# A tuned attention and mixing kernel: another hand-written order for the steps of its first two units

## The chip, the cores and the metric

One core of a Trainium2 chip runs the whole program in one launch. The metric is the device time of that launch in microseconds (us), as the median over several runs. The runs of the kernel before took 1000.03 to 1002.81 us, with a median of 1001.09 us.

## The reference

Three blocks follow each other. Only the first two are touched by the change.

```python
# 1: attention within chunks of 64, batch 8, 8 heads, sequence 576, head width 64
scores = q_c @ k_c.T / sqrt(64);  attn = softmax(scores);  out = attn @ v_c
# 2: the heads side by side give x (8, 576, 512); x_prev is x one step earlier
xk = mu_k * x + (1 - mu_k) * x_prev;  xr = mu_r * x + (1 - mu_r) * x_prev
k = relu(xk @ w_k)                        # 512 -> 1024
v = (k * k) @ w_v                         # 1024 -> 512
x2 = sigmoid(xr @ w_r) * v
# 3: four causal attention experts over x2 with a top-2 gate, width 64 each
```

## The kernel before

**Tiles and units.** Blocks 1 and 2 run as one pipeline. The 4608 positions (batch times sequence) are cut into 36 tiles of 128 for the attention and into 12 units of 384 for the mixing. Two neighbouring tiles make a pair: pair 0 is tiles 0 and 1, the seventh pair (pair 6) is tiles 12 and 13. The units are counted from 0, so the third unit is unit 2. Tiles from 12 on are loaded in 32 by 32 blocks (eight DMAs for a tile of q or of k) and transposed by VectorE; earlier tiles are loaded by one or two DMAs and transposed by TensorE.

**Precision.** Each float32 operand of a mixing product is split into a high and a low part, and each term is three matmuls (lines 95 to 97). One product step is 12 matmuls of 128x384.

**The order.** The scheduler does not choose the order of this part. Two lists of steps, START (line 21) for units 0 and 1 and TWO_UNITS (line 46) for each later two units, are walked by `follow` (line 495), and `in_line` (line 485) ties each instruction to the one before it on its engine. So the place of a step in the list is its place in the queue of every engine that it uses, SP's DMA queue too. An engine waits at the head of its queue for whatever that instruction still needs. The change is in START alone. The steps, as the lists name them:

- `L A G B H O` i: load a 512 KB piece of the weights on SP (L420), then split it into high and low: A on ScalarE (L426), G on VectorE (L430 and L431), B on VectorE (L435), H on GpSimd (L84), O on VectorE (L446). Pieces 0 to 3 are w_r, 4 to 11 w_k, 12 to 19 w_v. Pieces 4 and later share two staging buffers; one is free again after a B.
- `lq lk lv` t: load a tile of q, k or v on SP (L151 and L158, L166 and L174). Two buffers each; the v buffers of a pair are free after `V` of that pair, the q and k buffers after the tile's transposition.
- `Tq Tk Tp` t: transpose on TensorE (L187), or on VectorE (L197) for q and k from tile 12 on; `Eq Ek Ep`: copy out of PSUM on ScalarE (L192).
- `S X U E Z Y V W` j: attention of pair j. S (L211, L214) and V (L267, L270) are TensorE's; X (L224), U (L230), Z and Y are VectorE's; E and W are ScalarE's.
- `a b c d`, with `r` or `k`, u,g: the four stages of one shift of unit u (xr or xk), on ScalarE (L304), VectorE (L308), ScalarE (L315), VectorE (L319). They share two buffers.
- `r s` u,m: product with w_r, sigmoid. `k K J` u,m: product with w_k, three ScalarE instructions from L364 on (relu, square, high part), low part on VectorE (L370). `v y z x D` u,m: product with w_v in two halves, multiplication, split and store. The products of r, k and v share three PSUM banks.

TWO_UNITS follows START at once. Its first steps, for units 2 and 3 and from tile 12 on, are

```python
TWO_UNITS = """
Tq1 Tq0 lq2 Tk1 k0,0 Tk0 prev1 ar1,3 ak1,0 k0,1 br1,3 K0,0 bk1,0 lk2 cr1,3 k0,2 J0,0 K0,1 dr1,3 ar1,0 J0,1 k0,3 K0,2
```

so there `k0,0` is unit 2's first product with w_k, and the four `T` steps transpose tiles 12 and 13 on VectorE. START has made unit 2's r products and its shifts already.

Of the kernel before, what the change touches and what calls it, by code (L numbers as in the profile page):

```python
# [18 lines left out]
F64_BIAS = 2.0 ** -112  # L19

START = """
L7 A7 G7 B7 L3 G3 L5 H7 O7 A3 B3 H3 lk0 L6 lq0 Tq0 L1 A5 G5 B5 L14 H5 lk1 Tk0 O3 A6 G6 B6 lq1 Eq0 L2 Tk1 H6 O5 G1 O6
A1 B1 A14 Ek1 G14 H1 O1 lk2 B14 H14 Ek0 G2 O14 Tq1 Eq1 S0 mu A2 B2 X0 H2 O2 lk3 L4 A4 Tk2 Ek2 U0 E0 G4 Z0 lq2 Tq2 lq3
Eq2 Tk3 lv1 B4 Y0 Tq3 L11 G11 H4 Ek3 Eq3 S1 X1 A11 B11 H11 Tp1 Ep1 U1 lv0 Tp0 O11 Ep0 lq5 Tq5 lq4 V0 O4 E1 Z1 Y1 W0 L0
Tq4 A0 lk5 G0 lk4 Tk5 L8 G8 Ek5 B0 Eq5 Eq4 H0 Tk4 Ek4 Tp3 Ep3 Tp2 Ep2 S2 X2 lv2 O0 lv3 L19 A8 V1 W1 prev0 U2 A19 G19
ar0,2 br0,2 ar0,0 br0,0 E2 Z2 cr0,2 dr0,2 lq7 Tq7 lk6 Tk6 Eq7 cr0,0 dr0,0 Y2 lq6 Tq6 Eq6 lk7 Tk7 Ek6 ar0,1 br0,1 ar0,3
Ek7 br0,3 cr0,1 lq8 Tq8 Tp4 B8 Ep4 lk8 S3 cr0,3 H8 Eq8 dr0,1 ak0,2 Tk8 Ek8 Tp5 lq9 Tq9 dr0,3 r0,0 r0,1 X3 bk0,2 lv5
ak0,1 Ep5 bk0,1 Eq9 U3 O8 ck0,2 ck0,1 lk9 Tk9 B19 H19 lv4 V2 dk0,1 dk0,2 E3 Z3 lq11 Tq11 s0,1 r0,2 r0,3 Ek9 S4 ak0,0
bk0,0 ak0,3 bk0,3 W2 prev1 ck0,3 ck0,0 L10 s0,3 G10 dk0,3 A10 s0,2 lk10 s0,0 dk0,0 k0,0 k0,1 k0,2 O19 L9 G9 B10 H10
ar1,0 lv7 br1,0 A9 B9 lk11 Tk11 lq10 Tq10 H9 Eq11 O10 L17 Y3 K0,0 O9 K0,1 J0,1 L18 cr1,0 dr1,0 A17 ar1,1 lk13 K0,2 G17  # L30
J0,0 ar1,2 A18 k0,3 Tp6 Ep6 br1,1 G18 k0,4 J0,2 lv6 k0,5 B18 H18 Tp7 cr1,1 K0,4 dr1,1 B17 O18 H17 J0,4 ar1,3 K0,3
br1,2 cr1,2 br1,3 k0,6 k0,7 cr1,3 K0,6 L13 A13 L12 O17 J0,3 K0,7 dr1,2 dr1,3 r1,0 r1,1 G13 A12 Ep7 B13 H13 Eq10 s1,0
L15 G12 B12 Ek11 V3 O13 J0,7 G15 s1,1 H12 O12 A15 W3 B15 L16 r1,2 Tk10 r1,3 A16 G16 Ek10 S5 s1,2 H15 O15 K0,5 B16 H16
lv9 ak1,1 J0,6 J0,5 s1,3 v0,0,0 O16 v0,0,1 ak1,3 bk1,3 X4 v0,1,0 v0,1,1 ck1,3 v0,2,0 v0,2,1 bk1,1 ck1,1 dk1,1 U4 ak1,0
E4 bk1,0 y0,1 z0,1 x0,1 D0,1 y0,0 dk1,3 ak1,2 bk1,2 ck1,0 dk1,0 v0,3,0 ck1,2 dk1,2 v0,3,1 k1,0 K1,0 z0,0 x0,0 y0,2
z0,2 D0,0 k1,1 K1,1 Z4 Y4 Tp9 Tp8 Ep8 y0,3 lv8 X5 J1,1 U5 k1,2 k1,3 x0,2 Ep9 K1,2 k1,4 k1,5 J1,2 D0,2 J1,0 K1,3 J1,3
K1,4 z0,3 x0,3 k1,6 k1,7 E5 J1,4 K1,5 K1,6 J1,5 K1,7 v1,0,0 J1,6 V4 W4 J1,7 v1,0,1 prev2 v1,1,0 ak2,1 D0,3 lv11 v1,1,1
v1,2,0 v1,2,1 Z5 Y5 Tp10 bk2,1 y1,0 ar2,2 br2,2 v1,3,0 cr2,2 v1,3,1 z1,0 y1,1 x1,0 D1,0 dr2,2 ar2,0 br2,0 ck2,1 dk2,1
cr2,0 dr2,0 ar2,3 br2,3 ar2,1 br2,1 Ep10 cr2,3 z1,1 x1,1 D1,1 Tp11 dr2,3 y1,2 z1,2 cr2,1 dr2,1 r2,0 r2,1 x1,2 ak2,3
bk2,3 ck2,3 dk2,3 s2,0 ak2,2 y1,3 ak2,0 s2,1 r2,2 r2,3 z1,3 lv10 Ep11 V5 s2,2 x1,3 D1,3 bk2,0 ck2,0 s2,3 bk2,2 ck2,2  # L40
lv13 lk12 D1,2 W5 lq13 lv12 lq12 dk2,0 dk2,2
""".split()

CH = 64
# [999 lines left out]
```

## Time and profile before

| | before |
|---|---|
| median of three runs | 1001.09 us |
| the profiled execution | 1000.0 us, of which its span 998.0 us |
| TensorE matmul busy | 946.5 us (95%) |
| VectorE, ScalarE, GpSimd busy | 670.2, 624.0, 192.2 us |
| span, DMA | 108.38 MB, mean 109 GB/s |

The execution's time stands beside the span that its trace covers; the 2 us between them lie outside the trace. Times in the rows count from the start of the span. PE is TensorE's matmul, DVE VectorE, ACT ScalarE, POOL GpSimd, SP the engine that issues most DMAs. A row names the line, the operation, the tile written and the tile read; "idle before" is what the engine waited just before that instruction and what ended the wait.

### The profile page before, as it was taken

What the parts mean: (1) busy time and instruction counts of PE and PEld (TensorE: products, weight loads), DVE (VectorE), ACT (ScalarE), POOL (GpSimd) and SP (SyncE); (2) the same over time, 40 slices, a digit from 0 to 9 for tenths busy, and PEclk for the clock granted to TensorE, in tenths of its full rate; (3) what the DMA queues carried; (4) which work ended last, traced back from release to release, by engine and by line L of the source; (5) the groups of instructions that cost most, each with busy time, mean ns of one, the idle gap of its engine ahead of it and who ended that gap; (6) DMA issues with size and microseconds to landing.
All of it is one profiled execution on the core that took longest, in us unless ns stands there. A gap on an engine that the chain in (4) does not pass through costs nothing.

```text
span 998.0 us, 21524 instructions
## 1 busy us (share of the span) xinstructions
PE 946.5 (95%) x8022; PEld 908.4 (91%) x8022; DVE 670.2 (67%) x1705; ACT 624.0 (63%) x1417; POOL 192.2 (19%) x336
## 2 busy tenths in 40 slices
PE   2699998699999999999999999999999999999997
PEld 2589998699999999999999999989989998998996
DVE  7899552565665557464747622688786787778885
ACT  3588364547675675657466924476675667567675
POOL 3112111020201111020202024323321233222101
PEclk9699999799999999999999999999999999999999
DMA  9875123453344334433413225565453645354312
GB/s 255 201 193 145 44 69 85 67 109 71 96 77 93 81 86 86 85 92 74 107 30 85 49 69 138 117 171 135 112 156 94 179 87 174 87 170 137 100 44 97
DMA packets 223408, 108.38 MB, mean 109 GB/s; under 512 B 187352, under 2 KB 199752, under 8 KB 223304
## 3 DMA queue, kind: packets, MB, share of 16 engines
q1 hardware_dynamic: 193032, 67.16, 29.7%
q0 software_dynamic: 30272, 39.86, 14.7%
q8 instruction: 63, 1.03, 0.4%
q14 instruction: 41, 0.34, 0.1%
HBM read 66.01 MB, written 28.38 MB: 95 GB/s over the span
## 4 chain that ended last, share of the span: by engine, by line
PE 84%; DVE 8%; DMA 3%; SPq 1%; ACT 1%; issue 1%; POOL 0%; ACTq 0%; POOLq 0%; DVEq 0%
PE mps L95 17%; PE mps L97 16%; PE mps L96 16%; PE pj L95 6%; PE pj L96 6%; PE pj L97 6%; PE Sps L747 4%; PE Tps L807 3%; PE AVps L840 2%; PE Tps L187 2%; PE AVps L836 2%; DMA st<-in_moe_w_k_dram 2%; PE PVps L267 1%; PE Sps L211 1%; DVE PTl L814 1%
## 5 line engine op out<-in xcount | busy, mean ns | idle before, releaser
L95 PE MATMUL mps<-xhk,wkh 128*128 128x384 f32 x384 | 131.9, 343 | 11.9 <-ACT r L364 11.9
L96 PE MATMUL mps<-xlk,wkh 128*128 128x384 f32 x384 | 129.9, 338 | 0.0
L97 PE MATMUL mps<-xhk,wkl 128*128 128x384 f32 x384 | 129.8, 338 | 0.0
L95 PE MATMUL mps<-kh,wvh 128*128 128x384 f32 x384 | 129.3, 338 | 0.0
L97 PE MATMUL mps<-kh,wvl 128*128 128x384 f32 x384 | 128.4, 334 | 0.0
L96 PE MATMUL mps<-kl,wvh 128*128 128x384 f32 x384 | 128.3, 334 | 0.0
L370 DVE TENSOR_TENSOR kl<-r,kh 128x384 fp32r<-128x384 f32 x96 | 54.0, 564 | 100.0 <-ACT kh L366 100.0
L759 ACT ACTIVATE P<-sm,nm 128x512 f32<-128x512 f32 (+3 forms) x144 | 83.7, 583 | 22.2 <-DVE nm L749 13.4
L84 POOL CAST x2d<-x2o 128x384 fp32r<-128x384 f32 x48 | 31.3, 653 | 316.1 <-DVE x2o L387 314.0
L749 DVE CUSTOM_DVE_ANT_0 sm<-Sps,mask 128x256 f32<-128x256 f32 (+4 forms) x160 | 74.8, 478 | 21.6 <-PE Sps L747 20.7
L95 PEld LDWEIGHTS mps<-xhk,wkh 128*128 128x128 f32 x384 | 73.0, 190 | 12.9 <-ACT r L364 12.5
L814 DVE TENSOR_TENSOR PTl<-Tps,PTh 128x512 fp32r<-128x512 f32 (+2 forms) x144 | 70.3, 506 | 5.8 <-ACT PTh L813 4.4
L96 PEld LDWEIGHTS mps<-xlk,wkh 128*128 128x128 f32 x384 | 73.0, 190 | 0.0
L97 PEld LDWEIGHTS mps<-xhk,wkl 128*128 128x128 f32 x384 | 72.9, 190 | 0.0
L95 PEld LDWEIGHTS mps<-kh,wvh 128*128 128x128 f32 x384 | 72.0, 188 | 0.7
L96 PEld LDWEIGHTS mps<-kl,wvh 128*128 128x128 f32 x384 | 72.1, 188 | 0.0
L97 PEld LDWEIGHTS mps<-kh,wvl 128*128 128x128 f32 x384 | 72.1, 188 | 0.0
L304 ACT ACTIVATE xa<-XT,mu 128x384 f32<-128x384 f32 x96 | 57.0, 615 | 23.4 <-DVE xlk L319 12.3
L308 DVE SCALAR_TENSOR_TENSOR xa<-XT,mu,xa 128x384 f32<-128x384 f32 x96 | 57.6, 621 | 18.4 <-ACT xa L304 18.1
L364 ACT ACTIVATE r<-mps 128x384 f32<-128x384 f32 x96 | 46.6, 485 | 34.5 <-PE mps L97 34.1
L813 ACT ACTIVATE PTh<-Tps 128x512 fp32r<-128x512 f32 (+2 forms) x144 | 61.7, 454 | 8.5 <-PE Tps L807 6.8
L95 PE MATMUL mps<-xhr,wrh 128*128 128x384 f32 x192 | 66.3, 345 | 0.0
(182 smaller groups left out, 2629.9 us busy)
## 6 DMA issues: line engine op xcount, KB each, us to landing
x2T<-x2d POOLq DMA_DIRECT2D x48, 384.0 KB, 2.8
x<-x2T POOLq DMA_DIRECT2D x32, 576.0 KB, 7.0
K<-Kph SPq DMA_DIRECT2D x64, 128.0 KB
out_dram<-o SPq DMA_DIRECT2D x32, 256.0 KB
ldk<-in_k_dram SPq DMA_DIRECT2D x192, 32.0 KB
ldq<-in_q_dram SPq DMA_DIRECT2D x192, 32.0 KB
ldv<-in_v_dram SPq DMA_DIRECT2D x21, 256.0 KB
st<-in_moe_w_k_dram SPq DMA_DIRECT2D x8, 512.0 KB
```

Source lines behind the costliest of these rows:

```text
L95: nc.tensor.matmul(out=out, lhsT=ah, rhs=bh, start=first and i == 0, stop=False)
L96: nc.tensor.matmul(out=out, lhsT=ah, rhs=bl, start=False, stop=False)
L97: nc.tensor.matmul(out=out, lhsT=al, rhs=bh, start=False, stop=last and i == n - 1)
L304: nc.scalar.activation(out=a, in_=XT[u][:, g, :, :SEG], func=ACTF.Copy, scale=mu1[:, w, g:g + 1])
L308: nc.vector.scalar_tensor_tensor(a, XT[u][:, g, :, 1:], mu[:, w, g:g + 1], a, op0=ALU.mult, op1=ALU.add)
L364: nc.scalar.activation(out=r, in_=MB.pop(("k", u, m)), func=ACTF.Relu)
L370: eng(nc, CFG["klo"][u >= CFG["nearly"]]).tensor_tensor(o.lo, K2.pop((u, m)), f32(o.hi), op=ALU.subtract)
L747: issued = nc.tensor.matmul(out=pp[:, :w], lhsT=x, rhs=y[:, a:a + w], start=n == 0, stop=n == len(terms) - 1)
L749: nc.vector.tensor_tensor_reduce(out=sm[:, a:a + w], in0=pp[:, :w], in1=mk[:, :w], op0=ALU.add, op1=ALU.min, scale=-scale, scalar=3e38, ac ...
L759: nc.scalar.activation(out=x[:, :nk], in_=sm[:, :nk], func=ACTF.Exp, scale=-1.0, bias=nm[:, :1], accum_out=z)
L813: nc.scalar.activation(out=h, in_=src, func=ACTF.Copy)
L814: nc.vector.tensor_tensor(l, src, f32(h), op=ALU.subtract)
```

## The change

The list START is written in another order. It has the same 502 steps, each once; no step is added, dropped or altered, and everything after the list is the same. The first and the last lines of the two versions:

```diff
-L7 A7 G7 B7 L3 G3 L5 H7 O7 A3 B3 H3 lk0 L6 lq0 Tq0 L1 A5 G5 B5 L14 H5 lk1 Tk0 O3 A6 G6 B6 lq1 Eq0 L2 Tk1 H6 O5 G1 O6
...
-bk2,3 ck2,3 dk2,3 s2,0 ak2,2 y1,3 ak2,0 s2,1 r2,2 r2,3 z1,3 lv10 Ep11 V5 s2,2 x1,3 D1,3 bk2,0 ck2,0 s2,3 bk2,2 ck2,2
-lv13 lk12 D1,2 W5 lq13 lv12 lq12 dk2,0 dk2,2
+L3 G3 A3 L0 A0 B3 G0 H3 O3 B0 L4 G4 H0 O0 L1 A4 B4 H4 L15 G15 O4 A15 lq0 B15 lk1 G1 H15 O15 A1 B1 H1 Tk1 L7 G7 A7 lk0
...
+ak2,1 bk2,1 ck2,1 dk2,1 lq12 z1,1 x1,1 D1,1 Ep10 ak2,3 y1,3 s2,0 s2,1 r2,2 V5 r2,3 bk2,3 ck2,3 ak2,0 lv12 bk2,0 dk2,3
+z1,3 x1,3 D1,3 lv13 ck2,0 W5 s2,2 s2,3 dk2,0
```

**First place: SP's queue at the end of the list.** Before, the last loads of START and the first of TWO_UNITS; v tiles 11, 10 and 13, k 12, q 13, v 12, q 12, and then q 14 (k tile 13 stands far ahead of them):

```order
L174 DMA ldv_1790<-in_v_dram 64x4x64 x4
L174 DMA ldv_1985<-in_v_dram 64x4x64 x4
L166 DMA ldv_2034<-in_v_dram 64x8x64 x2
L151 DMA ldk_2037<-in_k_dram 32x8x32 x8
L151 DMA ldq_2050<-in_q_dram 32x8x32 x8
L166 DMA ldv_2059<-in_v_dram 128x8x64
L151 DMA ldq_2061<-in_q_dram 32x8x32 x8
L151 DMA ldq_2076<-in_q_dram 32x8x32 x8
```

Now, from v tile 9 on: v 9, k 12, v 8, q 13, two pieces of expert weights, v 10 and 11, k 13, q 12, v 12 and 13:

```order
L174 DMA ldv_1307<-in_v_dram 64x4x64 x4
L151 DMA ldk_1393<-in_k_dram 32x8x32 x8
L174 DMA ldv_1442<-in_v_dram 64x4x64 x4
L151 DMA ldq_1576<-in_q_dram 32x8x32 x8
L566 DMA wst_7275<-in_moe2_wq_dram 128x4x64
L566 DMA wst_7279<-in_moe2_wq_dram 128x4x64
L174 DMA ldv_1826<-in_v_dram 64x4x64 x4
L174 DMA ldv_1922<-in_v_dram 64x4x64 x4
L151 DMA ldk_1955<-in_k_dram 32x8x32 x8
L151 DMA ldq_1969<-in_q_dram 32x8x32 x8
L166 DMA ldv_2055<-in_v_dram 128x8x64
L166 DMA ldv_2062<-in_v_dram 64x8x64 x2
```

The q and k tiles of pair 6 now stand ahead of the two v tiles of that pair, k 12 and q 13 ahead of v 10 and 11 as well; k 13 has come down behind v 11.

**Second place: SP's queue ahead of the first mixing product.** Before, v tiles 2 and 3, a piece of w_v (19), then q 7, k 6, q 6, k 7, q 8, k 8, q 9, the last load that stands ahead of `r0,0` on TensorE as a transposition:

```order
L174 DMA ldv_504<-in_v_dram 64x4x64 x4
L174 DMA ldv_510<-in_v_dram 64x4x64 x4
L420 DMA st_515<-in_moe_w_v_dram 128x1024
L158 DMA ldq_581<-in_q_dram 128x8x64
L158 DMA ldk_588<-in_k_dram 128x8x64
L158 DMA ldq_600<-in_q_dram 128x8x64
L158 DMA ldk_609<-in_k_dram 128x8x64
L158 DMA ldq_627<-in_q_dram 128x8x64
L158 DMA ldk_642<-in_k_dram 128x8x64
L158 DMA ldq_697<-in_q_dram 128x8x64
```

Now, from v tiles 3 and 2 on: k 7, q 7, q 6, k 6, a piece of w_k (6), q 9, k 8, q 11:

```order
L174 DMA ldv_520<-in_v_dram 64x4x64 x4
L174 DMA ldv_525<-in_v_dram 64x4x64 x4
L158 DMA ldk_570<-in_k_dram 128x8x64
L158 DMA ldq_590<-in_q_dram 128x8x64
L158 DMA ldq_603<-in_q_dram 128x8x64
L158 DMA ldk_619<-in_k_dram 128x8x64
L420 DMA st_637<-in_moe_w_k_dram 128x1024
L158 DMA ldq_641<-in_q_dram 128x8x64
L158 DMA ldk_696<-in_k_dram 128x8x64
L158 DMA ldq_713<-in_q_dram 128x8x64
```

The last transposition ahead of `r0,0` is now that of q tile 11, and a piece of weights stands three loads ahead of it.

**Third place: VectorE at the end of the list.** Before, the end of unit 2's k shifts, the four transpositions of pair 6 and the first step of unit 3's shifts:

```order
L308 SCALAR_TENSOR_TENSOR xa_1955<-XT_1259,mu_93,xa_1955 128x384
L308 SCALAR_TENSOR_TENSOR xa_1950<-XT_1259,mu_93,xa_1950 128x384
L319 TENSOR_TENSOR xlk_1887<-xa_1955,xhk_1886 128x384
L319 TENSOR_TENSOR xlk_1887<-xa_1950,xhk_1886 128x384
L197 STREAM_TRANSPOSE qT_2072<-ldq_2050 128x512
L197 STREAM_TRANSPOSE qT_2074<-ldq_2061 128x512
L197 STREAM_TRANSPOSE kT_2085<-ldk_1010 128x512
L197 STREAM_TRANSPOSE kT_2100<-ldk_2037 128x512
L308 SCALAR_TENSOR_TENSOR xa_2104<-XT_1755,mu_93,xa_2104 128x384
```

Now, from the last x2o of unit 1 on:

```order
L387 TENSOR_TENSOR x2o_1985<-mps_1880,sig_1258 128x384
L308 SCALAR_TENSOR_TENSOR xa_1983<-XT_1831,mu_93,xa_1983 128x384
L308 SCALAR_TENSOR_TENSOR xa_2053<-XT_1831,mu_93,xa_2053 128x384
L319 TENSOR_TENSOR xlk_1861<-xa_1983,xhk_1860 128x384
L396 TENSOR_TENSOR x2d_1987<-x2o_1985,x2d_1987 128x384
L319 TENSOR_TENSOR xlk_1861<-xa_2053,xhk_1860 128x384
L197 STREAM_TRANSPOSE qT_2072<-ldq_1576 128x512
L197 STREAM_TRANSPOSE qT_2074<-ldq_1969 128x512
L197 STREAM_TRANSPOSE kT_2085<-ldk_1955 128x512
L197 STREAM_TRANSPOSE kT_2100<-ldk_1393 128x512
```

The four transpositions stand behind the last shift as before, and the x2o and x2d steps of unit 1 have come down among the last shifts.

## Rows read from the trace of the kernel before

**Rows 1.** Windows of the run, us: busy us (instructions) of each engine, granted clock, DMA share, GB/s.
```profile
0.00:57.65 57.65, 30.43 (x484) 25.33 (x485) 47.57 (x78) 30.30 (x55) 12.45 (x22) 0.82 0.91 220
57.65:163.00 105.35, 104.71 (x960) 102.31 (x959) 75.52 (x131) 70.34 (x139) 19.54 (x30) 1.00 0.39 106
182.60:187.70 5.10, 5.10 (x17) 5.10 (x18) 2.75 (x6) 4.94 (x11) 0.00 (x0) 0.53 0.42 65
188.00:600.00 412.00, 412.00 (x3770) 404.03 (x3770) 244.77 (x438) 256.63 (x495) 52.04 (x88) 1.00 0.37 79
```

**Rows 2.** Who waited for whom on PE, 60 to 600 us: total, times, longest.
```profile
PE mps L95 <- ACT r L364: 11.9, 2, 11.3
```

**Rows 3.** Timeline of PE: start us, us, what, [idle before <-releaser].
```profile
57.65 0.42 PE L95 MATMUL mps<-xhr,wrh 128*128 128x384 f32 x1
...
161.63 1.16 PE L270 MATMUL PVps<-PT,ldv 64*64 64x64 f32 x64
...
162.72 0.44 PE L95 MATMUL mps<-xhk,wkh 128*128 128x384 f32 x1
...
170.97 0.34 PE L97 MATMUL mps<-xhk,wkl 128*128 128x384 f32 x1
...
182.56 0.69 PE L95 MATMUL mps<-xhk,wkh 128*128 128x384 f32 x1 [11.26 <-ACT r L364]
...
187.49 0.33 PE L95 MATMUL mps<-xhk,wkh 128*128 128x384 f32 x1
```

**Rows 4.** Timeline of DVE at the end of the first list.
```profile
162.67 0.56 DVE L319 TENSOR_TENSOR xlk<-xa,xhk 128x384 fp32r<-128x384 f32 x1 [1.52 <-ACT xhk L315]
174.65 0.71 DVE L197 STREAM_TRANSPOSE qT<-ldq 128x512 f32<-128x512 f32 x1 [11.42 <-DMA ldq<-in_q_dram]
179.18 0.71 DVE L197 STREAM_TRANSPOSE qT<-ldq 128x512 f32<-128x512 f32 x1 [3.82 <-DMA ldq<-in_q_dram]
...
181.00 1.11 DVE L308 SCALAR_TENSOR_TENSOR xa<-XT,mu,xa 128x384 f32<-128x384 f32 x2
```

**Rows 5.** Timeline of ACT at the end of the first list.
```profile
181.61 0.52 ACT L315 ACTIVATE xhr<-xa 128x384 fp32r<-128x384 f32 x1 [14.90 <-DVE xa L308]
```

**Rows 6.** Timeline of SP's DMA queue.
```profile
35.02 1.53 SPq L420 DMA_DIRECT2D st<-in_moe_w_k_dram  x1
...
137.30 6.45 SPq L174 DMA_DIRECT2D ldv<-in_v_dram  x8
...
162.38 1.27 SPq L166 DMA_DIRECT2D ldv<-in_v_dram  x2
163.71 5.00 SPq L151 DMA_DIRECT2D ldk<-in_k_dram  x8
168.75 3.90 SPq L151 DMA_DIRECT2D ldq<-in_q_dram  x8
...
173.19 7.98 SPq L151 DMA_DIRECT2D ldq<-in_q_dram  x16
```

**Rows 7.** Windows of 25 us at the start, columns as in rows 1.
```profile
0.00:25.00 25.00, 6.68 (x86) 5.21 (x87) 19.33 (x31) 9.32 (x14) 8.63 (x16) 0.97 0.98 255
25.00:50.00 25.00, 16.96 (x304) 14.29 (x303) 21.25 (x36) 14.59 (x27) 2.95 (x5) 0.69 0.87 201
```

**Rows 8.** Timeline of DVE: its first instruction, the four of one piece of weights, and a pair's maxima.
```profile
5.11 0.43 DVE L430 TENSOR_SCALAR st<-st 128x512 int32<-128x512 int32 x1 [5.11 <-DMA st<-in_moe_w_k_dram]
...
42.53 0.43 DVE L430 TENSOR_SCALAR st<-st 128x512 int32<-128x512 int32 x1 [2.14 <-DMA st<-in_moe_w_k_dram]
42.99 0.69 DVE L431 SCALAR_TENSOR_TENSOR st<-st 128x512 int32<-128x512 int32 x1
43.60 0.69 DVE L435 SCALAR_TENSOR_TENSOR cz<-cz,st 128x512 int32<-128x512 int32 x1
44.99 1.29 DVE L224 TENSOR_REDUCE m<-Sps 128x8 f32<-128x512 f32 x2 [0.70 <-PE Sps L214]
46.19 0.68 DVE L446 TENSOR_TENSOR wrl<-cz,wrh 128x512 fp32r<-128x512 f32 x1
```

More of the change, by code (lines that the diff above doesn't have):

```diff
@@ L21 @@
 START = """
-L7 A7 G7 B7 L3 G3 L5 H7 O7 A3 B3 H3 lk0 L6 lq0 Tq0 L1 A5 G5 B5 L14 H5 lk1 Tk0 O3 A6 G6 B6 lq1 Eq0 L2 Tk1 H6 O5 G1 O6
[L23 to L36, printed above, removed]
@@ L37 @@
-K1,4 z0,3 x0,3 k1,6 k1,7 E5 J1,4 K1,5 K1,6 J1,5 K1,7 v1,0,0 J1,6 V4 W4 J1,7 v1,0,1 prev2 v1,1,0 ak2,1 D0,3 lv11 v1,1,1
-v1,2,0 v1,2,1 Z5 Y5 Tp10 bk2,1 y1,0 ar2,2 br2,2 v1,3,0 cr2,2 v1,3,1 z1,0 y1,1 x1,0 D1,0 dr2,2 ar2,0 br2,0 ck2,1 dk2,1
-cr2,0 dr2,0 ar2,3 br2,3 ar2,1 br2,1 Ep10 cr2,3 z1,1 x1,1 D1,1 Tp11 dr2,3 y1,2 z1,2 cr2,1 dr2,1 r2,0 r2,1 x1,2 ak2,3
-bk2,3 ck2,3 dk2,3 s2,0 ak2,2 y1,3 ak2,0 s2,1 r2,2 r2,3 z1,3 lv10 Ep11 V5 s2,2 x1,3 D1,3 bk2,0 ck2,0 s2,3 bk2,2 ck2,2
-lv13 lk12 D1,2 W5 lq13 lv12 lq12 dk2,0 dk2,2
+L3 G3 A3 L0 A0 B3 G0 H3 O3 B0 L4 G4 H0 O0 L1 A4 B4 H4 L15 G15 O4 A15 lq0 B15 lk1 G1 H15 O15 A1 B1 H1 Tk1 L7 G7 A7 lk0
@@ new lines @@
+Tk0 Tq0 Ek0 O1 B7 H7 L5 G5 Eq0 A5 Ek1 O7 B5 H5 lq1 L2 G2 Tq1 Eq1 S0 mu O5 X0 A2 B2 U0 E0 lk2 Tk2 lq2 Tq2 Eq2 L13 A13
+G13 lk3 Tk3 Z0 B13 Y0 H13 lq3 Tq3 L11 G11 Ek2 O13 Ek3 Eq3 S1 X1 U1 H2 O2 Tp0 lv0 lv1 Ep0 Tp1 Ep1 A11 B11 H11 E1 Z1 O11
+lq4 Tq4 Eq4 lk5 V0 Tk5 lk4 lq5 L9 Tk4 Ek4 Y1 G9 Ek5 Tq5 Eq5 S2 X2 U2 A9 L8 G8 W0 Tp2 Ep2 A8 Tp3 Ep3 E2 Z2 lv3 lv2 B9
+V1 W1 lk7 Tk7 Ek7 prev0 ar0,0 Y2 br0,0 ar0,1 br0,1 B8 H8 lq7 Tq7 Eq7 cr0,0 dr0,0 lq6 cr0,1 dr0,1 Tq6 Eq6 O8 ar0,3
+ar0,2 lk6 br0,3 Tk6 Ek6 br0,2 Tp4 Ep4 L6 G6 lq9 cr0,3 dr0,3 cr0,2 dr0,2 Tp5 Ep5 S3 X3 ak0,2 bk0,2 A6 lk8 U3 Tq9 Tk8
@@ new lines @@
+Ek8 lq11 Tq11 lk9 lv5 r0,0 r0,1 B6 Tk9 Eq9 ak0,3 bk0,3 lv4 V2 ck0,2 dk0,2 E3 Z3 s0,0 ck0,3 dk0,3 r0,2 r0,3 lq10 Tq10
+Y3 ak0,0 bk0,0 Ek9 L16 ak0,1 bk0,1 H6 O6 L19 W2 ck0,0 dk0,0 Tp6 ck0,1 dk0,1 Tp7 s0,2 lq8 Tq8 prev1 ar1,1 s0,3 A19 s0,1
+G19 ar1,3 Ep7 k0,0 k0,1 H9 O9 B19 br1,1 G16 k0,2 Eq8 S4 Ep6 cr1,1 lk10 Tk10 H19 O19 K0,0 br1,3 dr1,1 L10 G10 A10 B10
+ar1,0 J0,0 H10 K0,1 br1,0 k0,3 A16 O10 J0,1 k0,4 Eq10 B16 X4 K0,2 J0,2 k0,5 cr1,0 dr1,0 lv7 lk11 Tk11 K0,3 U4 J0,3
+ar1,2 k0,6 K0,5 k0,7 br1,2 cr1,2 H16 O16 L12 A12 G12 lv6 V3 J0,5 cr1,3 dr1,3 K0,4 L17 dr1,2 B12 r1,0 A17 H12 L14 G17
@@ new lines @@
+B17 K0,6 O12 H17 J0,6 Ek11 L18 Eq11 r1,1 O17 G14 s1,0 A14 s1,1 B14 H14 Ek10 ak1,3 G18 A18 r1,2 r1,3 O14 K0,7 lv9 B18
+ak1,2 S5 H18 v0,0,0 J0,7 s1,3 J0,4 s1,2 O18 v0,0,1 v0,1,0 lk12 v0,1,1 v0,2,0 v0,2,1 X5 lv8 U5 y0,0 v0,3,0 v0,3,1 bk1,3
+z0,0 ck1,3 bk1,2 ck1,2 dk1,2 ak1,1 E4 y0,1 x0,0 D0,0 bk1,1 z0,1 dk1,3 ck1,1 dk1,1 E5 ak1,0 y0,2 bk1,0 x0,1 ck1,0 dk1,0
+k1,0 K1,0 k1,1 K1,1 Z4 Y4 Tp9 z0,2 Z5 k1,2 D0,1 lq13 J1,0 K1,2 J1,1 x0,2 D0,2 Ep9 k1,3 K1,3 y0,3 J1,2 J1,3 k1,4 Tp8
+k1,5 k1,6 K1,4 J1,4 z0,3 x0,3 k1,7 K1,5 J1,5 Ep8 V4 K1,6 J1,6 K1,7 J1,7 v1,0,0 v1,0,1 v1,1,0 D0,3 v1,1,1 v1,2,0 v1,2,1
@@ L42 @@
+lv10 W3 y1,0 W4 prev2 ak2,2 bk2,2 Y5 Tp11 ar2,2 br2,2 z1,0 x1,0 D1,0 ck2,2 cr2,2 dr2,2 dk2,2 ar2,0 br2,0 cr2,0 dr2,0
+ar2,1 Ep11 y1,2 v1,3,0 v1,3,1 y1,1 ar2,3 z1,2 x1,2 br2,3 cr2,3 br2,1 cr2,1 Tp10 dr2,3 lv11 D1,2 dr2,1 r2,0 r2,1 lk13
+ak2,1 bk2,1 ck2,1 dk2,1 lq12 z1,1 x1,1 D1,1 Ep10 ak2,3 y1,3 s2,0 s2,1 r2,2 V5 r2,3 bk2,3 ck2,3 ak2,0 lv12 bk2,0 dk2,3
+z1,3 x1,3 D1,3 lv13 ck2,0 W5 s2,2 s2,3 dk2,0
 """.split()
```

## The prediction

> **What bounds the kernel now.** I read the stretches first. From 188 to 600 us TensorE (PE) is busy for 412.00 of 412.00 us at the full clock [rows 1], so whatever is saved ahead of 188 us reaches the end one for one, and nothing behind it needs a look. From the first mixing product at 57.65 us to 163 us it is busy for 104.71 of 105.35 us [rows 1, 3]. Ahead of that lies the warm-up, where PE is busy for 30.43 us of 57.65 and VectorE (DVE) for 47.57 [rows 1]. Then I read who PE waited for: from 60 to 600 us there are only two waits, 11.9 us together, both of `mps` L95 on ScalarE's relu L364, the longest 11.3 [rows 2]. The timeline puts that one behind four products of unit 2, which start at 162.72 us; the last matmul starts at 170.97 and the next at 182.56 [rows 3].
>
> The relu is only the messenger. ScalarE (ACT) had idled 14.90 us, waiting for DVE's xa [rows 5]. DVE had finished the third unit's last shift at 163.2 us and then waited 11.42 and 3.82 us for the q tiles of the seventh pair; only at 181.00 did it come to the xa of unit 3 [rows 4]. The tiles were late because SP issued them late. The v tile ahead of them went out at 162.38, just after the products V5 (161.63) that free its buffer, and the 8 + 8 + 8 transfers behind it took SP until about 177 us [rows 3, 6].
>
> **The stall at the end of the list goes: -13.7 us.** Ahead of the wait a matmul takes 0.175 us (48 from 162.72 to 171.14). Behind it 15 matmuls take from 182.56 to 187.49, at a granted clock of 0.53, which is the 1.2 GHz level; then they run at full speed again [rows 1, 3]. At 0.175 us the matmul that began at 187.49 would have begun at 170.97 + 16 x 0.175 = 173.8. So wait and slow clock cost 13.7 us. The Trainium skill, TensorE: Matmul & The Clock Gate, section Part 1, says that the array's clock is throttled unless activity releases it; the trace agrees, with the 0.53 behind the 11.26 us wait. By that rule the 2.3 us of slow matmuls go with the wait, and a longer wait of PE right ahead of `r0,0` would bring them back there.
>
> Are the tiles really there in time? In the new order k 12 and q 13 stand behind v 9 and v 8, freed by V3, and k 13 and q 12 behind v 10 and v 11, freed by V4. Eight transfers for two such v tiles took SP 6.45 us, eight for a k tile 5.00 and eight for a q tile 3.90 [rows 6]; with some 2 us to land (the last issue of q 12 near 177, its use at 179.18 [rows 4, 6]) the pair has landed about 17.4 us after V4. On PE there stand between V4 and unit 2's first product the eight halves of unit 1's v products, two groups of four transpositions, four r products and V5: 12 x 12 x 0.175 + 0.9 + 1.1 = 27.2 us. That leaves 10 us to spare. DVE's four transpositions (0.71 us each at most) then find their data. v 12 and v 13 still wait for V5, but behind them in SP's queue stands only q 14, as before.
>
> **The third unit's shifts.** The last one ends DVE's list, and `k0,0` of unit 2 needs it. Behind PE's second r product six small instructions follow each other between ACT and DVE (sigmoid, xhk, xa, xa, xhk, xlk), 0.52 to 0.56 us each [rows 4, 5], with perhaps 0.15 us for each hand-over: some 4.1 us. PE meanwhile has two r products and V5, 2 x 2.1 + 1.1 = 5.3 us. Cost nothing, with 1.2 us of cover; if an instruction or two more got in between, it would show as a wait at that place.
>
> **The warm-up: +1.0 us (-2.5 to +5.1).** PE's work ahead of `r0,0` is the same by count (25 groups of transpositions, four pairs' scores, two pairs' products), so what is left behind `r0,0` is the same too, and only its start matters. It has two bounds. DVE has 13 pieces of weights begun ahead of the unit's last r shift where it had 12, and 12 and 11 finished where it had 11 and 10: one L430, L431, L435 and L446 more, 0.43 + 0.69 + 0.69 + 0.68 = 2.5 us [rows 8]. It starts at 5.11 us with the first load. Without any idle time it would be through at 5.1 + 47.6 + 2.5 = 55.2 us; with the 10.1 us of idle time that it has now, at 60.1. The loads are the other bound. Ahead of q 11 stand 13 pieces of 0.524 MB and 23 tiles of 0.262 MB, together 12.84 MB; now it is 12 pieces and 23 tiles ahead of and with q 9. The first 25 us move 255 GB/s, 6.37 MB, and the next 25 move 201, 5.03 MB [rows 7]; the other 1.44 MB at 201 GB/s land at 57.2, and with the transposition `r0,0` starts at 57.9. I take 58.65, between 57.9 and 60.1 and nearer the loads. The late end: piece 6 waits on SP until DVE has joined piece 9 (L435), by the same count 40.6 us into its queue, at 50.7 with the same idle time; a piece took 7.5 us from issue to use (35.02 to 42.53 [rows 6, 8]), then three tiles of 1.3 us and the transposition: 62.8.
>
> **The products of units 0 and 1: +1.0 us (0 to +3).** From `r0,0` to the first k product DVE has 10.5 us of work under 12.0 us of PE (9.9 under 11.8 before), and from there to unit 1's first r product 17.3 under 19.9 (16.7 under 18.5), counted from the two lists with 0.5 to 0.6 us for a shift step [rows 4] and rows 8 for the rest. The ratio is nearly the same, so no great wait is to be expected; but the list was woven for other moments. The one wait of this kind costs 0.6 us now (11.9 less 11.3 [rows 2]). I take 1.0.
>
> **Sum.** -13.7 + 1.0 + 1.0 = -11.7 us. The profiled execution took 1000.0 us, so 988.3; the median of the runs lies 1.1 above it, so 989.4 us. With both late ends: -13.7 + 5.1 + 3.0 = -5.6. With both early ones: -13.7 - 2.5 = -16.2.
>
> **Rivals.**
> - DVE becomes the bound of the units' products. It keeps its idle time (+2.5), and what it has more of ahead of unit 1's r product (a piece's first two instructions, a pair's maxima of 1.29 us and its subtraction, about as long [rows 8]: 3.7 us) all falls on PE. For it: from 57.65 to 163 us DVE is busy 75.5 us, most of that early [rows 1]. Against: the cover worked out above grows too. -13.7 + 2.5 + 3.7 + 1.0 = -6.5: 994.6 us. Chance 0.10.
> - The loads do not bind. Then DVE runs without a gap and `r0,0` starts at 55.2, with no later wait: 984.9 us. Against: DVE's 10.1 us of gaps. Beside it the Trainium skill, DMA: Bandwidth & Descriptors, section Specifications, gives about 358 GB/s of HBM for one core; by that the 12.84 MB would land at an estimated 36 us. The 255 and 201 GB/s of the trace disagree, and decide. Chance 0.08.
> - The change does not do what it says: the pair is still late, because V4, which frees the v buffers, comes over 10 us later against unit 2's first product than counted above. Then the stall stays: some 1001 us. Chance 0.04.
> - Slower: the loads get slower still. Piece 6 and the three tiles behind it are the gate to `r0,0`, and every microsecond there reaches the end. It decides once `r0,0` starts after 57.65 + 13.7 - 1.0 + 3.0 = 73.3 us, that is if the 6.47 MB behind the first 25 us move at under 136 GB/s. At 125 GB/s `r0,0` starts at 77.4, and the run takes 1008.2 us. Against it are the 201 GB/s. Chance 0.05.
>
> **How the numbers follow.** The forecast has 0.73. 0.3%, about 3 us, is what a measurement of this kernel can tell from no change. The forecast's own ends, -16.2 to -5.6 from 1001.1, with half a microsecond for the scatter of runs, give 984.4 to 996.0; the first two rivals lie inside. Faster: 0.73 + 0.10 + 0.08 = 0.91. Same 0.04, slower 0.05.
>
> **What would show it.** PE's waits between 60 and 600 us lose the 11.3 us; DVE's L197 at the end of the list shows no wait on `ldq` or `ldk`; the granted clock stays at 1.00 through unit 2's first products. The first `mps` matmul starts between 55 and 63 us. From it to unit 2's first k product lie 105 to 108 us. I am wrong if a wait of several microseconds stands at one of these places: `r0,0` on q 11, `k0,0` or `r1,0` on a DVE low part, or unit 2's `k0,0` on the last shift.

## The result, and the profile after

| | before | after |
|---|---|---|
| median of four runs | 1001.16 us | 984.64 us |
| lowest to highest | 1000.03 to 1002.81 | 984.44 to 985.38 |
| the profiled execution, its span | 1000.0, 998.0 us | 984.82, 982.7 us |

The ratio after to before is 0.9835, with a 95% interval of 0.9818 to 0.9852: 1.65% faster, 16.5 us by the medians and 15.2 by the profiled executions (the profiled one of before lay 1.1 below its median). The forecast was 989.4 us, with a range of 984.4 to 996.0.

The windows of after, cut at its own landmarks, answer to [rows 1] and [rows 7] (us; busy us and instructions of PE, PEld, DVE, ACT, POOL; granted clock, DMA share, GB/s):

```profile
0.00:58.22 58.22, 29.14 (x485) 24.14 (x485) 50.92 (x83) 31.29 (x56) 12.62 (x22) 0.88 0.91 227
58.22:163.00 104.78, 104.30 (x957) 101.93 (x956) 75.16 (x129) 70.59 (x138) 19.98 (x31) 1.00 0.42 107
172.00:177.00 5.00, 5.00 (x31) 5.00 (x30) 2.18 (x5) 4.37 (x9) 0.00 (x0) 1.00 0.43 66
188.00:600.00 412.00, 412.00 (x3716) 404.33 (x3715) 239.57 (x428) 257.00 (x495) 54.66 (x93) 1.00 0.37 80
...
0.00:25.00 25.00, 7.16 (x88) 5.70 (x88) 20.17 (x32) 8.90 (x13) 8.14 (x16) 1.00 0.97 264
25.00:50.00 25.00, 15.91 (x304) 13.06 (x304) 23.07 (x38) 15.10 (x29) 3.14 (x5) 0.80 0.85 195
```

Right behind unit 2's first four products, where before showed 0.53, the clock is at 1.00. PE's waits from 60 to 600 us, which were 11.9 us [rows 2], are now one line:

```profile
PE PVps L270 <- DMA ldv<-in_v_dram: 0.3, 1, 0.3
```

The timeline of PE, at the places of [rows 3]: the first mixing product, V5, unit 2's first k product, and the matmul that stood behind the 11.26 us wait.

```profile
58.22 0.42 PE L95 MATMUL mps<-xhr,wrh 128*128 128x384 f32 x1
...
160.10 1.16 PE L270 MATMUL PVps<-PT,ldv 64*64 64x64 f32 x64
...
163.38 0.34 PE L95 MATMUL mps<-xhk,wkh 128*128 128x384 f32 x1
...
171.70 0.34 PE L95 MATMUL mps<-xhk,wkh 128*128 128x384 f32 x1
```

The timeline of DVE at the end of the list, for [rows 4]: the last shift (L319), the four transpositions (L197) and unit 3's first xa (L308). The waits of 11.42 and 3.82 us on `ldq` are gone.

```profile
161.03 0.55 DVE L319 TENSOR_TENSOR xlk<-xa,xhk 128x384 fp32r<-128x384 f32 x1
161.50 1.30 DVE L197 STREAM_TRANSPOSE qT<-ldq 128x512 f32<-128x512 f32 x2
162.73 1.26 DVE L197 STREAM_TRANSPOSE kT<-ldk 128x512 f32<-128x512 f32 x2
164.61 1.15 DVE L308 SCALAR_TENSOR_TENSOR xa<-XT,mu,xa 128x384 f32<-128x384 f32 x2 [0.62 <-ACT xa L304]
```

The timeline of SP's queue, for [rows 6]: v 10 and 11, k 13 and q 12 are issued by 150 us; v 12 and 13 still wait for V5, and only q 14 stands behind them.

```profile
135.79 6.09 SPq L174 DMA_DIRECT2D ldv<-in_v_dram  x8
141.92 4.12 SPq L151 DMA_DIRECT2D ldk<-in_k_dram  x8
146.09 3.97 SPq L151 DMA_DIRECT2D ldq<-in_q_dram  x8
160.85 1.78 SPq L166 DMA_DIRECT2D ldv<-in_v_dram  x3
```

Where the time went, from the starts of the same matmuls in PE's timeline (the 577th, 769th, 2977th and last of the 4296 of lines 95 to 97; the 577th is the one that stood behind the wait):

| stretch, us | before | after | difference |
|---|---|---|---|
| start to the first mixing product | 57.65 | 58.22 | +0.57 |
| from there to unit 2's first k product | 105.07 | 105.16 | +0.09 |
| from there to the 577th (the wait) | 19.84 | 8.32 | -11.52 |
| 577th to 769th (the slow clock) | 38.66 | 36.32 | -2.34 |
| 769th to 2977th | 421.21 | 420.87 | -0.34 |
| 2977th to the last | 351.15 | 349.39 | -1.76 |

They add up to -15.30 us.

### The profile page after: what moved, and what is told of

Same layout as the page of the kernel before. It is cut to its first block, busy times and chain, and to the rows that moved or that the text cites. A ratio compares the mean times of both kernels' runs of the same rounds, so it can differ in the third digit from the quotient of the medians.

```text
span 982.7 us, 21527 instructions
## 1 busy us (share of the span) xinstructions
PE 942.1 (96%) x8022; PEld 904.9 (92%) x8022; DVE 670.9 (68%) x1705; ACT 625.2 (64%) x1417; POOL 192.4 (20%) x336
## 4 chain that ended last, share of the span: by engine, by line
PE 86%; DVE 8%; DMA 3%; ACT 1%; issue 1%; SPq 1%; POOL 0%; ACTq 0%; POOLq 0%; DVEq 0%
PE mps L95 17%; PE mps L97 17%; PE mps L96 17%; PE pj L95 6%; PE pj L96 6%; PE pj L97 6%; PE Sps L747 4%; PE Tps L807 3%; PE AVps L840 2%; PE AVps L836 2%; PE Tps L187 2%; DMA st<-in_moe_w_v_dram 2%; PE PVps L267 1%; PE Sps L211 1%; DVE PTl L814 1%
## 5 line engine op out<-in xcount | busy, mean ns | idle before, releaser
L308 DVE SCALAR_TENSOR_TENSOR xa<-XT,mu,xa 128x384 f32<-128x384 f32 x96 | 58.4, 628 | 18.8 <-ACT xa L304 18.6
```

The lines of the kernel that those rows point to most:

```text
L308: nc.vector.scalar_tensor_tensor(a, XT[u][:, g, :, 1:], mu[:, w, g:g + 1], a, op0=ALU.mult, op1=ALU.add)
```

## The experiments

**Before, unaltered, once more.** It tells what two profiles of one kernel differ by.

> The kernel before, unaltered, to see which of its waits repeat. In its first profile two waits stand behind 860 us that the changed kernel has not: 0.9 us of Sps L747 on GpSimd's Ql and 0.6 us of Sps on VectorE's nm; with them the gain grows from 13.5 us at 620 us to 15.3 at the end. If they belong to the scatter of executions, they are gone or elsewhere here and the matmul clock of the two traces differs at the end by another amount (13 to 15 us). If the first list's order causes them, they stand at the same places with the same sizes.

Measured: 999.13 us. The first product starts at 57.37, the wait is 11.8 us (two, the longest 11.2), and the stretch behind the 2977th matmul takes 350.14 us, 1.0 less than in the first profile of the same kernel. Of the two late waits named above, the one on GpSimd's Ql (0.88 us at 922.74 in the first profile) is gone here. A wait on it of 0.68 to 0.80 us also shows in profiles of both orders further down (before with three loads moved; after with a piece of weights moved, and with v tiles early), so it is scatter. The other stands at the same place with the same 0.56 us. PE's timeline of before has it as

```profile
867.90 0.39 PE L747 MATMUL Sps<-K,Q 128*128 128x256 f32 x1 [0.56 <-DVE nm L749]
```

All four profiles with the order of before have this wait, and none of the eight with the order of after or a variant of it. So of the 1.76 us in the last line of the table about an us is the scatter of executions, and this wait comes with the order. Why it does was not tried.

**Before, with three loads alone moved.** In the order of before k 12, q 13 and q 12 go ahead of the two v tiles that wait for V5; the warm-up and the shifts stay.

```diff
-... z1,3 lv10 Ep11 V5 s2,2 x1,3 D1,3 bk2,0 ck2,0 s2,3 bk2,2 ck2,2
-lv13 lk12 D1,2 W5 lq13 lv12 lq12 dk2,0 dk2,2
+... z1,3 lv10 lk12 lq13 lq12 Ep11 V5 s2,2 x1,3 D1,3 bk2,0 ck2,0
+s2,3 bk2,2 ck2,2 lv13 D1,2 W5 lv12 dk2,0 dk2,2
```

> The order of before, with only three loads moved on SP: k 12, q 13 and q 12 go out before v 13 and v 12. My theory (the stall is the loads' lateness and nothing else): the pair has landed by some 158 us, the 11.3 us wait of PE and the 2.3 us of slow matmuls behind it go, the first product still starts at 57.6 to 57.7, and the run takes 13.2 to 13.9 us less than before, about 987.5. The rival (the third unit's shifts are next in line, and the new order is needed to bring them forward): the last shift ends at 163.2 us as before and PE finds a new wait of 1 to 5 us in unit 2's first products, so 989 to 993.

Measured: 987.08 us (985.08 to 987.42), ratio 0.9855 (0.9833 to 0.9877). The timeline of DVE shows the last shift end at 164.0, with the four transpositions behind it at once, and no wait of PE moves into that place; all that PE's waits from 60 to 600 us still show is this line, the short wait, in unit 1's k products, that before has as well:

```profile
PE mps L95 <- ACT r L364: 0.6, 1, 0.6
```

DVE's timeline:

```profile
163.44 0.56 DVE L319 TENSOR_TENSOR xlk<-xa,xhk 128x384 fp32r<-128x384 f32 x1 [1.52 <-ACT xhk L315]
163.91 1.30 DVE L197 STREAM_TRANSPOSE qT<-ldq 128x512 f32<-128x512 f32 x2
165.13 1.27 DVE L197 STREAM_TRANSPOSE kT<-ldk 128x512 f32<-128x512 f32 x2
```

From unit 2's first k product to the 769th matmul it takes 44.76 us, 13.74 less than before: the three loads alone bring the whole stall term. The shifts, which this kernel leaves as they were, bring no wait there. The first product starts at 58.42, not at the 57.6 to 57.7 expected.

**After, with the same three loads put back late.** v 12 goes back behind q 13 with them, as in before; k 13 stays early.

```diff
-... v0,1,0 lk12 v0,1,1 ... D0,1 lq13 J1,0 ... dk2,1 lq12 z1,1 ... ak2,0 lv12 bk2,0 dk2,3
-z1,3 x1,3 D1,3 lv13 ck2,0 W5 s2,2 s2,3 dk2,0
+... v0,1,0 v0,1,1 ... D0,1 J1,0 ... dk2,1 z1,1 ... ak2,0 bk2,0 dk2,3
+z1,3 x1,3 D1,3 ck2,0 lv13 lk12 W5 lq13 lv12 lq12 s2,2 s2,3 dk2,0
```

> The changed order, with k 12, q 13 and q 12 put back behind v 13 and v 12, in the order in which they stood before. My theory: the queue behind V5 takes 17.5 us again as before (161.63 to 179.18), V5 starts at 160.1, so the last tile is used at 177.6 and PE goes on 3.4 us later, at 181.0; its four products end at 171.8, so a wait of 9 us and 2.3 us of slow matmuls come back: 11 to 12 us more than the changed kernel, about 996. The rival (the rest of the order has made the stall shorter or harmless): under 6 us more, below 990.

Measured: 997.29 us (996.26 to 999.32), ratio to before 0.997 (0.9957 to 0.9983), 12.65 above after. The wait is back on the same instruction, as PE's timeline shows:

```profile
180.69 0.69 PE L95 MATMUL mps<-xhk,wkh 128*128 128x384 f32 x1 [9.04 <-ACT r L364]
```

In DVE's timeline it has the same cause, the q tiles:

```profile
172.56 0.71 DVE L197 STREAM_TRANSPOSE qT<-ldq 128x512 f32<-128x512 f32 x1 [11.20 <-DMA ldq<-in_q_dram]
177.30 0.71 DVE L197 STREAM_TRANSPOSE qT<-ldq 128x512 f32<-128x512 f32 x1 [4.03 <-DMA ldq<-in_q_dram]
```

And the window behind the wait is at the slow clock (columns as above):

```profile
180.69:183.69 3.00, 3.00 (x9) 3.00 (x10) 1.60 (x4) 2.90 (x7) 0.00 (x0) 0.50 0.44 68
```

**After, with half of the pair late.** Only k 13 and q 12 go behind v 13, so that the wait is shorter.

```diff
-... r2,1 lk13 ak2,1 bk2,1 ck2,1 dk2,1 lq12 z1,1 ... lv13 ck2,0 W5 s2,2 s2,3 dk2,0
+... r2,1 ak2,1 bk2,1 ck2,1 dk2,1 z1,1 ... lv13 lk13 lq12 ck2,0 W5 s2,2 s2,3 dk2,0
```

> The order of after with only half of the seventh pair put late again: k 13 and q 12 stand behind v 13, k 12 and q 13 stay where after has them. Theory (time goes one for one with how late the last of the four tiles lands): v 13 is issued until 162.6 us, k 13 takes SP 5.0 and q 12 3.9 more, q 12 lands about 173.6, and 3.4 us later (transpositions, xa, relu's turn, as before from 179.18 to 182.56) TensorE goes on, at about 177.0 instead of 171.8. So one wait of mps on the relu of 4 to 7 us, and behind it up to 2.3 us at the slow clock: 989 to 993 us. Rival 1 (only whole stalls of over 10 us bring the slow clock): the wait alone, 988.5 to 990.5, granted clock 1.00 in the 5 us behind it. Rival 2 (two tiles fit into the cover that is left): no wait, 984 to 986.

Measured: 993.98 us (992.12 to 994.53), ratio to before 0.9921 (0.9895 to 0.9947), and 9.75 above after in the same series. PE's timeline:

```profile
178.75 0.69 PE L95 MATMUL mps<-xhk,wkh 128*128 128x384 f32 x1 [5.91 <-ACT r L364]
```

DVE's timeline, where one q tile has landed and the other not:

```profile
162.48 0.70 DVE L197 STREAM_TRANSPOSE qT<-ldq 128x512 f32<-128x512 f32 x1
175.37 0.71 DVE L197 STREAM_TRANSPOSE qT<-ldq 128x512 f32<-128x512 f32 x1 [12.18 <-DMA ldq<-in_q_dram]
```

The window behind the wait:

```profile
178.75:181.75 3.00, 3.00 (x9) 3.00 (x10) 1.61 (x4) 2.91 (x7) 0.00 (x0) 0.50 0.42 65
```

A wait of 5.91 us brings the slow clock as well; the first rival falls, and so does the second. The time lies just above the expected 989 to 993: its first product starts at 58.89, 0.9 later than in after's profile of that series.

**A piece of weights and a q tile moved out of the warm-up of after.** Piece 13 goes behind piece 16, q 11 behind the first products. It takes 2.3 us of DVE work and two loads away from ahead of the first product.

```diff
-... Eq2 L13 A13 G13 lk3 Tk3 Z0 B13 Y0 H13 lq3 Tq3 L11 G11 Ek2 O13 Ek3 ... Ek8 lq11 Tq11 lk9 lv5 r0,0 r0,1 B6 ... B16 X4
+... Eq2 lk3 Tk3 Z0 Y0 lq3 Tq3 L11 G11 Ek2 Ek3 ... Ek8 lk9 lv5 r0,0 r0,1 lq11 Tq11 B6 ... B16 L13 G13 A13 B13 H13 O13 X4
```

> The changed order, with w_v's piece 13 loaded and split only behind the join of piece 16 instead of in the warm-up, and q tile 11 loaded and transposed behind the second r product instead of ahead of the first. My theory (VectorE and the loads bound the warm-up together): VectorE has 2.3 us less ahead of the last r shift and two loads fewer stand ahead of the first product, so it starts 1.5 to 2.5 us earlier than 58.2, at 55.7 to 56.7; if VectorE keeps up in the products of units 0 and 1, the run is 1.5 to 2.5 us faster, 982 to 983. The rival (VectorE is the bound up to the first v product): the 2.3 us come back as a wait of PE between 75 and 102 us, and the time stays at 984 to 985.5.

Measured: 984.24 us (983.26 to 987.72), ratio to before 0.983 (0.9809 to 0.9852): no gain over after. The first product starts at 57.69, where 55.7 to 56.7 was expected. The time is the one that the rival named, but its wait is not there: between 75 and 102 us PE waits once, 0.25 us. What the earlier start gains goes at 64 us, where PE waits 1.09 us ahead of V2. What the timeline of PE shows in the middle of the warm-up is V1, waiting for its v tiles one after the other:

```profile
44.98 0.30 PE L270 MATMUL PVps<-PT,ldv 64*64 64x64 f32 x2 [1.23 <-DMA ldv<-in_v_dram]
45.73 0.33 PE L270 MATMUL PVps<-PT,ldv 64*64 64x64 f32 x2 [0.46 <-DMA ldv<-in_v_dram]
47.21 1.15 PE L270 MATMUL PVps<-PT,ldv 64*64 64x64 f32 x60 [1.15 <-DMA ldv<-in_v_dram]
```

DVE's timeline shows the xa that needs V1's output wait behind it:

```profile
51.25 1.15 DVE L308 SCALAR_TENSOR_TENSOR xa<-XT,mu,xa 128x384 f32<-128x384 f32 x2 [1.49 <-ACT xa L304]
```

The DVE work that was taken away became idle time: DVE's waits from 25 to 58 us are 4.1 us, and 2.0 in after. The loads slowed too. Two loads fewer are 0.79 MB, 3.9 us at the 201 GB/s of [rows 7], but the first 50 us now move fewer bytes (columns as above):

```profile
0.00:25.00 25.00, 6.97 (x85) 5.56 (x86) 18.63 (x31) 8.80 (x13) 7.96 (x16) 1.00 0.95 244
25.00:50.00 25.00, 16.63 (x304) 13.31 (x303) 21.75 (x36) 13.26 (x25) 1.46 (x4) 0.76 0.82 187
```

Three kernels then tried to bring V1 forward.

**V tiles 3 and 2 ahead of two pieces of weights.**

```diff
-lq4 Tq4 Eq4 lk5 V0 Tk5 lk4 lq5 L9 Tk4 Ek4 ... E2 Z2 lv3 lv2 B9
+lq4 V0 Tq4 Eq4 lk5 Tk5 lk4 lq5 lv3 lv2 L9 Tk4 Ek4 ... E2 Z2 B9
```

> The order of after with two moves in the warm-up: V0 goes ahead of the transposition of q 4 on TensorE, and on SP v 3 and v 2 go ahead of the weight pieces 9 and 8. Theory (the way to the first product runs over V1, which waits for v 3 and v 2, which wait for V0 behind a late q 4): V0 starts near 34.5 us instead of 37.2, v 3 and v 2 are issued from about 35 instead of 38.4, V1 ends some 3 us sooner, and r0,0 starts at 55 to 57 us instead of 58.2: 981.5 to 984.0. Rival (pieces 9 and 8, now issued some 3 to 4 us later, hold VectorE and with it the shifts just as long): r0,0 between 57.5 and 60, 984 to 987, with VectorE waiting on a DMA of weights near 40 us.

Measured: 990.04 us (989.13 to 990.62), ratio to before 0.9885 (0.9862 to 0.9907), 5.8 us above after in the same series. The v tiles go out 2.6 us sooner than in after's profile of that series, but the two pieces only at 42.00, DVE stands still for piece 9, and the first product starts at 62.31. The rival named that wait, but put the first product at 57.5 to 60 and the time at 984 to 987. SP's timeline:

```profile
35.69 6.21 SPq L174 DMA_DIRECT2D ldv<-in_v_dram  x8
42.00 1.02 SPq L420 DMA_DIRECT2D st<-in_moe_w_k_dram  x2
```

DVE's timeline:

```profile
46.47 0.43 DVE L430 TENSOR_SCALAR st<-st 128x512 int32<-128x512 int32 x1 [5.53 <-DMA st<-in_moe_w_k_dram]
```

**One piece ahead, one behind, with piece 13 and q 11 moved out as above.** V0 stands ahead of the transposition of q 4; piece 8 goes behind v 2, and its G8 and A8 behind the second xa shift.

```diff
-lq4 Tq4 Eq4 lk5 V0 Tk5 ... S2 X2 U2 A9 L8 G8 W0 Tp2 Ep2 A8 Tp3 ... lv3 lv2 B9 ... ar0,1 br0,1 B8
+lq4 V0 Tq4 Eq4 lk5 Tk5 ... S2 X2 U2 A9 W0 Tp2 Ep2 Tp3 ... lv3 lv2 L8 B9 ... ar0,1 br0,1 G8 A8 B8
```

> The order of the earlier run with piece 13 and q 11 behind the first product, and in it V0 ahead of the transposition of q 4 on TensorE, piece 8 behind v 2 on SP, and its first VectorE and ScalarE steps (G8, A8) behind the second xa shift. Theory (two things hold the first product at the same time, VectorE's work and the v tiles of V1; only with both eased does it come sooner): v 3 and v 2 are issued some 2 us sooner, V1 runs near 45 us without a wait instead of until 48.4, r0,0 starts at 55.5 to 57.0 us: 982 to 983.5. Rival (the loads as a whole are the bound; what goes out sooner makes others later): r0,0 at 57.5 to 59, a wait on DMA st or ldq moved to another place, 984 to 986.

Measured: 985.98 us (985.42 to 986.73), ratio to before 0.9858 (0.9843 to 0.9873). V1 does run without waiting for a v tile, from 43.53 us on (in after most of it runs from 46.13), but the k tile behind it has not landed, DVE waits elsewhere, and the first product starts at 59.10. PE's timeline:

```profile
43.53 1.54 PE L270 MATMUL PVps<-PT,ldv 64*64 64x64 f32 x64 [0.36 <-ACT PT L192]
48.16 0.63 PE L187 MATMUL Tps<-ident,ldk 128*128 128x128 f32 x4 [3.08 <-DMA ldk<-in_k_dram]
...
59.10 0.52 PE L95 MATMUL mps<-xhr,wrh 128*128 128x384 f32 x1
```

**The same moves, with piece 13 and q 11 where after has them.**

> The order of after with the same moves of V0, piece 8, G8 and A8, but piece 13 and q 11 where after has them. Theory (VectorE, idle for under 2 us between 25 and 58 us, holds the first product alone): r0,0 at 57.5 to 58.9 as in the profiles of after, 983.5 to 985.5. Rival (the v tiles of V1 hold it alone): r0,0 at 55.5 to 57, 982 to 983.5.

Measured: 987.12 us (985.66 to 988.7), ratio to before 0.9864 (0.9848 to 0.988). The first product starts at 60.79; neither theory gave that. There, too, the transposition behind V1 waits for its k tile, 3.42 us. In all three, whatever goes out sooner makes something else late by as much or more, so no single tile holds the warm-up. What does is not shown. The amount loaded alone is not it: taking 0.79 MB away moved the first product by no more than half a microsecond, and fewer bytes went out in the same time instead. Nor does SP issue without a break: it waits for engines to free buffers, as in after up to 60 us (transpositions on PE, joins of pieces on DVE; total, times, longest, us):

```profile
SPq L158 <- PE Tps L187: 6.1, 3, 3.4
SPq L420 <- DVE cz L435: 4.5, 3, 2.7
```

**The three loads alone, and after, in one series.**

> The order of before with only k 12, q 13 and q 12 moved ahead of v 13, as in the earlier run of the same kernel, now in the same job as the order of after. Theory (all of the gain is the three loads; the rest of the new order brings nothing that can be measured): equal to the order of after within 1 us. Rival (the rest of the new order is worth the 1 to 3 us by which the two differed in the earlier runs, 987.1 against 984.6): 986 to 988 with the order of after at 984 to 985.

> The order of after unaltered, beside the three others on one chip: 984 to 985.5. Its profile tells how far the start of the first product scatters: theory 57.5 to 58.5 us; by the term of the prediction that the new warm-up starts it later, 58.2 or later.

Measured: 987.05 us (984.77 to 988.51), ratio 0.9851 (0.9826 to 0.9875), against 984.23 (982.98 to 987.28), ratio 0.983 (0.9806 to 0.9855). The ranges of the runs overlap, and the intervals too, but both medians lie where the rival put them, and they are not equal within 1 us. The two series together give 986.7 us on average for the three loads alone and 984.7 for after (nine runs each, standard error of the difference 0.6): the rest of the order is worth about 2 us more. Matmul by matmul the two profiles differ by 3.28 us at the last one: 0.92 at the first product, 1.46 up to unit 2's first k product, 0.13 from there to the 769th, 0.33 from there to the 2977th, 0.44 behind it. The first two scatter by as much between profiles of one order:

| order up to the end of the list | first product at, us | unit 2's first k product at, us |
|---|---|---|
| before (4 profiles) | 57.65, 57.37, 58.42, 58.91 | 162.72, 163.13, 163.49, 164.66 |
| after (4 profiles, two with loads put late) | 58.22, 57.99, 57.57, 58.89 | 163.38, 162.28, 163.16, 164.36 |

So of the order's other changes the 0.13, the 0.33 and, behind the 2977th, the 0.56 us wait named in the first experiment go with the order in every profile, about 1 us in all; where the other microsecond of the 2 lies is open (the 0.13: 44.76 in both profiles with the three loads alone, 44.63 and 44.64 in both of after; the 0.33: 421.20 or 421.21 in all four profiles with the order of before, 420.86 to 420.88 in all eight with that of after and its variants). From the 769th on the list is the same, PE is busy throughout up to the 2977th in both orders, and what makes the difference there was not tried. Nothing tried beats after.

## Why the prediction was right

**The stall: right, in size and cause.** -13.7 was predicted; -11.52 for the wait and -2.34 for the slow clock make -13.86 in after, and the three loads alone make -13.74. Put back, they bring the wait back. V4 and the pair's cover came out as counted: V4's buffers let SP start at 135.79, k 13 and q 12 are out at 150.06, and the first transposition, at 161.50, finds its data. The pair had 11 us to spare from its last issue, with landing still in it.

**The third unit's shifts: right.** The last one ends at 161.58, 1.8 us ahead of unit 2's first k product (1.2 had been worked out). A hand-over had been taken at 0.15 us; in after's timelines ScalarE's part of the xa there runs until 159.53 and VectorE's starts at 159.56, 0.03 us later. The three loads alone, with the shifts of before, show no wait at that place either. There the last shift ends 0.5 us after the product has begun, but it is the third quarter's (dk2,2), which the product reads from its seventh matmul on; in after it is the first quarter's (dk2,0).

**The warm-up: near in size, which is not to be told from zero; the gate is not shown.** +1.0 was taken, +0.57 measured, and the means of the two rows above are 58.1 and 58.2. DVE's busy time rose from 47.57 to 50.92 us, 3.3 where 2.5 was counted, but its idle time fell from 10.1 to 7.3, so the bound with the old idle time (60.1) was too late. As forecast, q 11 stood last ahead of the first product. In the first profile of after its transposition waits 0.33 us for it; in the second profile, shown behind it, it does not wait:

```profile
57.83 0.63 PE L187 MATMUL Tps<-ident,ldq 128*128 128x128 f32 x4 [0.33 <-DMA ldq<-in_q_dram]
```

```profile
57.64 0.60 PE L187 MATMUL Tps<-ident,ldq 128*128 128x128 f32 x4
```

The loads moved 264 and then 195 GB/s, and the bound worked out from 255 and 201 gave 57.9. (The 358 GB/s of the Trainium skill, DMA: Bandwidth & Descriptors, section Specifications, is not reached in after either.) That they bind by their amount is not shown, and the kernel with piece 13 and q 11 moved out speaks against it: the same working with two loads fewer gives an estimate of 54.0 for its first product, and it came at 57.69. So the 57.9 came near by luck as much as by its cause. The rival by which DVE runs without a gap (55.2) falls, since DVE still idles 7.3 us, and the slower one too: no gate after 73 us.

**The products of units 0 and 1: over-sized.** +1.0 was taken, +0.09 measured, the low end of its 0 to +3. The two profiles of after differ there by 0.9 us, so the size is not to be told from zero. Of DVE's growing load nothing fell on PE: it waits 0.3 us there, for a v tile, where before it waited 0.6. The rival in which DVE bounds these products falls with it.

**What the sum left out.** -11.7 was predicted, -15.2 measured between the profiled executions (-15.3 at their last matmul). The two terms above make 1.3 us of the difference, the stall 0.2. The rest is behind the stall, where nothing was expected: -0.34 up to the 2977th matmul, and -1.76 behind it. Of the 1.76, 0.88 us is the wait on Ql, which comes and goes in profiles of both orders, and 0.56 us the wait on nm, which stands in every profile of the order of before and in none of after's (the stretch takes 350.14 to 351.15 us in the order of before, 349.39 to 350.53 in that of after and its variants). So the failed step is the one that reads from the busy windows that nothing behind 188 us needs a look: PE shows 412.00 us busy of 412.00 in both orders, and yet the 2208 matmuls from the 769th on take 0.34 us less in after. The medians add 1.3: the profiled execution of before lay 1.16 below its median, that of after 0.18 above. The result lies only 0.2 us inside the range's low end. By the medians the change is -16.5, 0.3 beyond the sum's early end of -16.2, and the half microsecond added for scatter brings it in; that part is luck.

## What to carry to other kernels

A queue that issues in order makes every load behind a waiting one late: look at what the head of the queue waits for, and put ahead of it what does not need that. Three loads moved so brought 13.7 us, the whole of the stall; all 502 steps in a new order brought 15.2 by the profiles and 16.5 by the medians. In a stretch where many loads, buffers and engines wait for each other, as in this warm-up, moving a pair's v tiles forward only moved the wait, in each of the three kernels that did it.

## What was not expected of the hardware

The slow clock behind a wait cost nearly the same for waits of 5.9 to 11.3 us; shorter ones were not tried at this place. From the 577th to the 769th matmul it takes 36.32 us without a wait (36.34 and 36.31 in two other profiles). With one, it takes:

| kernel | wait, us | 577th to 769th, us | more than 36.32 |
|---|---|---|---|
| after, half of the pair late | 5.91 | 38.41 | 2.09 |
| after, three loads late | 9.04 | 38.80 | 2.48 |
| before, again | 11.2 | 38.62 | 2.30 |
| before | 11.26 | 38.66 | 2.34 |

The granted clock right behind the wait is 0.50 in both new cases, the 1.2 GHz level. So a wait of 6 us cost 8, and one of 11 us cost 13.6: halving the wait saved little more than the wait's own half.
